# Retention layer and serf MLP on one core: two reorderings of the weight conversion and one of a scaling step

## The chip, the core and the metric

The kernel runs on one NeuronCore of a Trainium2 chip. Its time is the device time in microseconds; lower is better. The engines are named as the profile names them: PE (TensorE matmuls), PEld (TensorE weight loads), DVE (VectorE), ACT (ScalarE), POOL (GpSimd) and SP (SyncE, which issues nearly all of the DMAs here).

## The reference, cut to what matters

First a recurrent retention layer on q, k, v of shape (4, 8, 768, 64), then a two-layer MLP on its output seen as 3072 tokens by 512. Shortened:

```python
for t in range(S):                       # retention, per batch and head
    state = gamma * state + outer(k[t], v[t])
    y[t] = scale * q[t] @ state
x = y.transpose(0, 2, 1, 3).reshape(3072, 512)
h = x @ w_in                             # 512 x 2048, float64 in memory
g = h * erf(softplus(h))
out = g @ w_out                          # 2048 x 512, float64 in memory
```

The two weight matrices arrive as float64 and there is no float64 arithmetic in the kernel, so the kernel rebuilds a float32 from the two 32-bit words of every number.

## The kernel before

**Retention by chunks.** The sequence is cut into chunks of 128 positions, 24 in all (six for each batch). For chunk j the functions, with their short names, are: `ret_scale` (K_, one DVE multiplication of q and k by decay factors, L401), `ret_transpose` (T, PE transposes at L416 into two PSUM tiles, which ACT copies at L422 to qT and kT), `ret_scores` (S_, L429, two PSUM tiles), `ret_mask` (M, two DVE multiplications at L441 that read the two score tiles), `ret_out` (O_, matmuls at L464, L469 and L478 into two PSUM tiles, which ACT copies at L483), and `ret_add` (A, DVE adds to the running state from PSUM, L596). After the first four chunks all of these PSUM tiles come from one pool, `ps_r`, which has two buffers: each function that writes two tiles takes over the two that the function in front of it filled, so it has to wait until they have been read.

**Weights by pieces.** The weights come in 16 pieces of 1 MB, numbered 0 to 15, in the order in0, in1, in2, in3, out0, out1, in4, in5, out2, out3, in6, in7, out4, out5, out6, out7. `conversion(n)` is a Python generator that turns piece n to float32. From piece 2 on it has five steps, each with one DVE instruction on 128x1024 elements:

- step 1: L211 cuts out the exponent, and ACT scales it with a Relu (L212);
- step 2: L215 cuts out the upper mantissa (into a tile that all pieces share);
- step 3: L220 adds the lower word;
- step 4: L223 joins the sign to what ACT wrote at L212, and issues the DMA of the piece that takes the same raw buffer;
- step 5: L229 multiplies the two and writes the float32 weights.

The exponent tiles alternate between even and odd n, so step 1 of piece n+1 may run while piece n is unfinished.

**Order.** The program is written out by hand: each engine runs its instructions in the order in which Python records them. `weights()` lists the conversion steps of all pieces in one sequence. Every function of the retention and of the MLP calls `pace(n)`, which records the next n steps of that sequence at that place; `need(...)` records as many as are wanted for a certain weight. `pace_around(n)` records n/2 steps, then what stands in the list `waiting`, then n/2 steps. So `pace` decides where the conversion's DVE instructions stand among the others.

**MLP.** For the first 512 tokens there are four groups g of four hidden tiles. `hidden(g, u)` is the first layer for one tile (L649, ACT copy at L652); `gate(g)` runs softplus and erf on ACT (L609, L619, each with a table load); `gated(g)` multiplies on DVE (L638); `project(g, tt)` is the second layer (L663). In group g the order is hidden(g, 0 to 3), gate(g), project(g-1, 0 to 3), with the steps for chunks 4 and 5 put between by the table `after`. `project(0, 0)` needs pieces 4 and 5 (out0 and out1): its first two hidden tiles use piece 4, the other two use piece 5. The later 2560 tokens run from `hidden_part` (L720) and `project_part` (L792), with block products that need fewer multiplications.

Of the kernel before, what the change touches and what calls it, by code (L numbers as in the profile page):

```python
# [45 lines left out]
def kernel(  # L46
# [85 lines left out]
    def w_in_of(ft, kk):  # L132
        half, s, i = ft // (2 * FG), ft % (2 * FG) // FG, ft % FG
        return w_in_sb[:, s, 2 * half + kk // 2, kk % 2, i * P : (i + 1) * P]

    def w_out_of(ft):
        half, s, i = ft // (2 * FG), ft % (2 * FG) // FG, ft % FG
        return w_out_sb[:, s, 2 * half : 2 * half + 2, i, :]
# [11 lines left out]
    pieces = [("in", 0), ("in", 1)]  # L150
# [4 lines left out]
    n_p = len(pieces)  # L155
# [23 lines left out]
    def load_pieces_after(n):  # L179
        for later in range(n + 1, n_p):  # L180
            if place[later] == place[n]:
                load_piece(later)
                break

    def conversion(n):

        which, i = pieces[n]
        half, s, at = i // 4, i % 4 // 2, i % 2  # L190

        for part in range(2) if n < 2 else (None,):
            words = raws[place[n]].bitcast(U32)
            if which == "in":
                f = slice(at * 2 * P, (at + 1) * 2 * P)
                if part is not None:
                    f = slice((at * 2 + part) * P, (at * 2 + part + 1) * P)
                to = w_in_sb[:, s, 2 * half : 2 * half + 2, :, f].rearrange("p d k f -> p (d k) f")
            else:
                to = w_out_sb[:, s, 2 * half : 2 * half + 2, at * 2 : at * 2 + 2, :].rearrange(  # L200
                    "p d f c -> p d (f c)"
                )
            words = words.rearrange("p (a b w) -> p a b w", a=to.shape[1], w=2)
            number, power = (
                x.rearrange("p (a b) -> p a b", a=to.shape[1]) for x in (numbers, powers[n % 2])
            )
            if part is not None:
                f = slice(part * P, (part + 1) * P)
                words, number, power = words[:, :, f], number[:, :, f], power[:, :, f]
            lo, hi = words[:, :, :, 0], words[:, :, :, 1]  # L210
            nc.vector.tensor_scalar(power, hi, 0x7FF00000, None, op0=ALU.bitwise_and)  # L211
            nc.scalar.activation(power, power, AF.Relu, bias=below, scale=8.0)  # L212
            if part is None:
                yield
            nc.vector.tensor_scalar(  # L215
                number, hi, 0xFFFFF, 1 << 20, op0=ALU.bitwise_and, op1=ALU.bitwise_or
            )
            yield
            numberf = number.bitcast(F32)
            nc.vector.scalar_tensor_tensor(numberf, number, 2.0**32, lo, op0=ALU.mult, op1=ALU.add)  # L220
            if part is None:
                yield
            nc.vector.scalar_tensor_tensor(  # L223
                power, hi, 1 << 31, power, op0=ALU.bitwise_and, op1=ALU.bitwise_or
            )
            if part != 0:
                load_pieces_after(n)
            yield
            nc.vector.scalar_tensor_tensor(  # L229
                to, numberf, 2.0**-52, power.bitcast(F32), op0=ALU.mult, op1=ALU.mult,  # L230
            )
            done.update((which, 2 * i + u) for u in (range(2) if part is None else (part,)))
            yield

    def sums(which, s):

        if which == "in":
            assert all(("hidden", 2 * FG + s * FG + u) in done for u in range(FG))
            x = {name: w_in_sb[:, s, at] for name, at in IN.items()}
            of = (("S1", "21", "22", 1), ("S2", "S1", "11", 0), ("S3", "11", "21", 0), ("S4", "12", "S2", 0))  # L240
        else:
            assert ("project", s) in done
            x = {name: w_out_sb[:, s, at] for name, at in OUT.items()}
            of = (("T1", "12", "11", 0), ("T2", "22", "T1", 0), ("T3", "22", "12", 0), ("T4", "21", "T2", 0))
        for to, a, b, plus in of:
            nc.vector.tensor_tensor(x[to], x[a], x[b], op=ALU.add if plus else ALU.subtract)
            yield
        done.add(("sums " + which, s))
# [3 lines left out]
    def weights():  # L252


        before = iter(())
        for n in range(n_p):
            now = conversion(n)
            if n > 5:
                next(now)
                yield  # L260
            for _ in before:
                yield
            before = now
            if n and pieces[n - 1] == ("out", 5):
                yield from sums("in", 0)
        yield from before

    def later_sums():
        for which, n in (("in", 1), ("out", 0), ("out", 1)):
            yield from sums(which, n)  # L270

    weight_steps = weights()
    last_steps = later_sums()
    room = -1000.0

    def pace(n):

        nonlocal room
        room += n
        while room >= 1:  # L280
            next(weight_steps, None)
            room -= 1

    def need(*what):
        nonlocal room
        while what not in done:
            if next(weight_steps, done) is done:
                next(last_steps)
            room -= 1
# [13 lines left out]
    for n in range(1, 4):  # L303
# [6 lines left out]
        out=causal, in_=causal, compare_op=ALU.is_ge, fill=0.0,  # L310
# [293 lines left out]
    def gate(g):  # L604


        name = "r" if g < 4 and g % 2 else "e"
        E[g] = act.tile([P, N], F32, name=name, bufs=1)
        nc.scalar.activation(E[g], HS[g], AF.Softplus)  # L609

        if g:
            gate_erf(g)
# [8 lines left out]
    waiting = []  # L621

    def pace_around(n):


        pace(n / 2)
        run(waiting)
        waiting.clear()
        pace(n / 2)

    def run(steps):
        for f, *args in steps:
            f(*args)
# [8 lines left out]
    def hidden(g, u):  # L642
        ft = g * FG + u
        if u == 0:
            HS[g] = act.tile([P, N], F32, name="h")
        need("in", ft)
        p = ps_h.tile([P, TCH], F32, name="hp")
        for kk in range(n_k):
            nc.tensor.matmul(  # L649
                p, w_in_of(ft, kk), XC[0][:, kk, :], start=(kk == 0), stop=(kk == n_k - 1)  # L650
            )
        nc.scalar.copy(HS[g][:, u * TCH : (u + 1) * TCH], p)  # L652
        done.add(("hidden", ft))

        pace_around(3.4 if g > 1 else 2.5)

    def project(g, tt):
        if g == 0 and tt == 0:
            O[0] = [ps_o.tile([P, d_model], F32, name=f"o{i}") for i in range(TT)]
        need("out", g * FG + FG - 1)  # L660
        for u in range(FG):
            ft = g * FG + u
            nc.tensor.matmul(  # L663
                O[0][tt].rearrange("p (d c) -> p d c", d=2),
                E[g][:, u * TCH + tt * P : u * TCH + (tt + 1) * P],
                w_out_of(ft),
                start=(ft == 0),
                stop=(ft == n_ft - 1),
            )
        if tt == TT - 1:  # L670
            done.add(("project", g))
        pace_around(3.4)
# [16 lines left out]
    def chunk_of(g):  # L689
        return TCH // SCH + (g - G0) // 2  # L690
# [116 lines left out]
    def put_part(m, step):  # L807
# [27 lines left out]
    K_, T, S_, M, O_, A = (  # L835
        ret_scale, ret_transpose, ret_scores, ret_mask, ret_out, ret_add
    )
# [6 lines left out]
    for j in range(JPC):  # L844
# [8 lines left out]
        else:  # L853
# [19 lines left out]
            ([(S_, 4)], [(M, 4)]),  # L873
        ],
        [
            ([(O_, 4), (load, 6)], [(A, 4), (K_, 5)]),
            ([(T, 5), (load, 7)], []),
            ([(S_, 5)], [(M, 5)]),
            ([(O_, 5)], [(A, 5)]),
# [8 lines left out]
    for g in range(G0):  # L888
        for u in range(FG):

            if g and u == (2 if g == 1 else 0):
                waiting.append((gated, g - 1))
            hidden(g, u)
            run(after[g][u][0])
            waiting.extend(after[g][u][1])
        gate(g)
        if g:
            for tt in range(TT):
                project(g - 1, tt)

# [76 lines left out]
    g, m = NG - 1, chunk_of(NG - 1)  # L979
# [55 lines left out]
```

## Time and profile before

| | |
|---|---|
| median of 6 runs | 692.99 us (692.12 to 694.92) |
| the profiled execution | 692.96 us |
| its span, first to last instruction | 691.2 us |
| busy: PE, DVE, ACT, POOL | 678.8, 384.4, 257.3, 6.6 us |
| mean granted TensorE clock | 0.997 |
| mean DMA rate over the span | 68 GB/s |

The profile is of one execution. Its timeline gives, for each group of equal instructions, start, duration, engine, line, output and inputs, and in brackets the idle time of the engine before it with what ended that idle time. Times in the timeline count from the span's start. [...]

### The profile page before, as it was taken

Reading aid. Unit: us, or ns where it says so; the run is one execution under the profiler, and the core shown is the slowest. Engines: PE = TensorE matmul, PEld = TensorE weight load, DVE = VectorE, ACT = ScalarE, POOL = GpSimd, SP = SyncE. Lnnn points to the kernel's source line nnn. Section 1 sums busy time; section 2 is a strip of 40 time slices with the busy share of each in tenths; the row PEclk is TensorE's granted clock in tenths of the full one; section 3 lists DMA queues with packets and bytes.
Section 4 is the critical chain, followed back from the end, with each engine's and each line's share of the span. In section 5 each row is a group of like instructions: output and inputs, shape, how many; then the busy total and the mean of one; then the engine's idle time right before and its main releaser. Section 6 shows DMA issues by size and latency. Waiting matters only on the chain.

```text
span 691.2 us, 14344 instructions
## 1 busy us (share of the span) xinstructions
PE 678.8 (98%) x6214; PEld 578.7 (84%) x6214; DVE 384.4 (56%) x591; ACT 257.3 (37%) x293; POOL 6.6 (1%) x21
## 2 busy tenths in 40 slices
PE   8898999999999999999999999999999999999997
PEld 7644454486999999999999999999999999999996
DVE  4698999564863653563455455544544553343224
ACT  3267262425144144243342341441441432423430
POOL 2000000010000000000000000000000000000000
PEclk9999999999999999999999999999999999999999
DMA  9999963202321321222222222322221210000000
GB/s 193 216 233 241 195 202 84 39 1 38 105 44 35 75 48 31 63 46 43 67 43 45 69 39 46 72 36 44 50 58 34 49 43 1 2 32 1 1 31 32
DMA packets 147216, 47.12 MB, mean 68 GB/s; under 512 B 135760, under 2 KB 136016, under 8 KB 147152
## 3 DMA queue, kind: packets, MB, share of 16 engines
q1 hardware_dynamic: 144640, 45.66, 30.4%
q8 instruction: 49, 0.80, 0.5%
q10 hardware_dynamic: 2512, 0.53, 0.5%
q14 instruction: 15, 0.12, 0.1%
HBM read 39.86 MB, written 6.29 MB: 67 GB/s over the span
## 4 chain that ended last, share of the span: by engine, by line
PE 94%; DVE 2%; SPq 1%; DMA 1%; ACT 1%; issue 1%; DVEq 0%
PE hp L720 36%; PE o L792 35%; PE o L663 8%; PE hp L649 7%; PE r L528 1%; DMA e<-in_q_dram 1%; PE hp L493 1%; PE o L564 1%; SPq L119 1%; SPq L122 1%; PE r L416 1%; PE r L469 1%; PE hp L543 1%; PE r L543 1%; PE r L429 0%
## 5 line engine op out<-in xcount | busy, mean ns | idle before, releaser
L720 PE MATMUL hp<-xs,w_in_sb 128*128 128x128 f32 x1280 | 149.8, 275 | 0.0
L720 PEld LDWEIGHTS hp<-xs,w_in_sb 128*128 128x128 f32 x1280 | 147.8, 192 | 1.6 <-issue 0.5
L792 PE MATMUL o<-w_out_sb,h 128*128 128x256 f32 x640 | 141.7, 379 | 0.0
L792 PEld LDWEIGHTS o<-w_out_sb,h 128*128 128x128 f32 x640 | 121.6, 190 | 16.5
L720 PE MATMUL hp<-xT,w_in_sb 128*128 128x128 f32 x960 | 113.7, 275 | 0.0
L720 PEld LDWEIGHTS hp<-xT,w_in_sb 128*128 128x128 f32 x960 | 111.9, 192 | 1.9 <-issue 1.0
L792 PE MATMUL o<-w_out_sb,e 128*128 128x256 f32 x480 | 112.1, 383 | 0.0
L638 DVE TENSOR_TENSOR e<-h,e 128x1024 f32<-128x1024 f32 x42 | 49.6, 1222 | 102.7 <-ACT e L619 102.7
L792 PEld LDWEIGHTS o<-w_out_sb,e 128*128 128x128 f32 x480 | 88.2, 190 | 11.6
L649 PE MATMUL hp<-xT,w_in_sb 128*128 128x512 f32 x128 | 56.6, 595 | 0.8 <-DVE w_in_sb L229 0.7
L745 DVE TENSOR_TENSOR h<-h,hp 128x512 f32<-128x512 f32 x20 | 13.7, 687 | 75.3 <-PE hp L720 75.3
L609 ACT ACT_TABLE_LOAD x24 | 30.8, 1283 | 61.1 <-issue 45.4
L649 PEld LDWEIGHTS hp<-xT,w_in_sb 128*128 128x128 f32 x128 | 23.8, 190 | 29.8 <-issue 27.3
L619 ACT ACTIVATE e<-e 128x2048 f32<-128x2048 f32 (+1 forms) x23 | 42.1, 1836 | 0.2
L609 ACT ACTIVATE e<-h 128x2048 f32<-128x2048 f32 x22 | 42.0, 1911 | 0.2
L733 DVE TENSOR_TENSOR h<-h,hp 128x512 f32<-128x512 f32 x20 | 13.8, 688 | 46.5 <-PE hp L720 46.5
L743 ACT COPY h<-hp 128x512 f32<-128x512 f32 x20 | 11.7, 585 | 60.3 <-PE hp L720 60.3
L738 ACT COPY h<-hp 128x512 f32<-128x512 f32 x20 | 11.7, 586 | 57.9 <-PE hp L720 57.9
L736 ACT COPY h<-hp 128x512 f32<-128x512 f32 x20 | 11.7, 585 | 55.3 <-PE hp L720 55.3
L619 ACT ACT_TABLE_LOAD x24 | 30.8, 1283 | 0.4
L582 ACT COPY xT<-r 128x256 f32<-128x256 f32 x32 | 10.4, 375 | 54.8 <-PE r L528 54.8
L663 PE MATMUL o<-w_out_sb,e 128*128 128x512 f32 x64 | 28.2, 595 | 2.3 <-DVE w_out_sb L229 2.3
(134 smaller groups left out, 660.7 us busy)
## 6 DMA issues: line engine op xcount, KB each, us to landing
w_out_sb<-in_moe_w_out_dram SPq DMA_DIRECT2D x14, 512.0 KB, 5.7
w_in_sb<-in_moe_w_in_dram SPq DMA_DIRECT2D x12, 512.0 KB, 12.0
kq<-in_k_dram SPq DMA_DIRECT2D x23, 256.0 KB, 3.8
v<-in_v_dram SPq DMA_DIRECT2D x23, 256.0 KB, 3.1
out_dram<-r SPq DMA_DIRECT2D x23, 256.0 KB, 3.4
kq<-in_q_dram SPq DMA_DIRECT2D x256, 16.0 KB, 1.8
kb<-in_k_dram SPq DMA_DIRECT2D x256, 16.0 KB, 1.7
w_out_sb<-in_moe_w_in_dram SPq DMA_DIRECT2D x4, 512.0 KB, 10.7
```

The lines of the kernel that those rows point to most:

```text
L543: nc.tensor.matmul(other[a][own, u % 2, D:] if crossed else pp[a][own, u % 2, t], V[j][t, 2 * u + r, :], AM[j][t, r, u, :D], start=crossed ...
L609: nc.scalar.activation(E[g], HS[g], AF.Softplus)
L619: nc.scalar.activation(E[g][:, half], E[g][:, half], AF.Erf)
L638: nc.vector.tensor_tensor(E[g][:, half], HS[g][:, half], E[g][:, half], op=ALU.mult)
L649: nc.tensor.matmul(p, w_in_of(ft, kk), XC[0][:, kk, :], start=(kk == 0), stop=(kk == n_k - 1))
L663: nc.tensor.matmul(O[0][tt].rearrange("p (d c) -> p d c", d=2), E[g][:, u * TCH + tt * P : u * TCH + (tt + 1) * P], w_out_of(ft), start=(f ...
L720: nc.tensor.matmul(bank[:, u, :], w_in_sb[:, s, IN[a], kk, u * P : (u + 1) * P], XS[m][b][:, kk, :], start=(p in (1, 2, 5) and u == 0 and ...
L733: nc.vector.tensor_tensor(h["11"], h["11"], flat, op=ALU.add)
L736: nc.scalar.copy(h["12"], flat)
L738: nc.scalar.copy(h["22"], flat)
L745: nc.vector.tensor_tensor(h["12"], h["12"], flat, op=ALU.add)
L792: nc.tensor.matmul(O[m][i][:, half, :], G[g][a][:, u * P : (u + 1) * P], w_out_sb[:, s, OUT[b], u, :], start=i not in started, stop=(s == ...
```

## The change

There are three edits.

1. `weights()` places step 1 of piece n+1 differently. Before, from piece 6 on, step 1 of a piece stood in front of all remaining steps of the piece before it (for piece 6: in front of all five steps of piece 5). Now step 1 of piece n+1 stands between step 3 and step 4 of piece n, from piece 6 (the seventh) on.
2. `hidden(g, u)` calls `pace_around` with 3.4 steps from group 1 on, where group 1 had 2.5.
3. The scaling of chunk 5, the sixth (`K_` for 5), leaves the list that follows `hidden(2, 0)` and is put in the list that follows `project(0, 1)`, so that it is recorded in `project(0, 2)`.

```diff
@@ weights()
-        before = iter(())
-        for n in range(n_p):
-            now = conversion(n)
-            if n > 5:
-                next(now)
+        pending = [conversion(n) for n in range(n_p)]
+        begun = 0
+        for n, steps in enumerate(pending):
+            for k, _ in enumerate(steps, start=begun):
                 yield
-            for _ in before:
-                yield
-            before = now
-            if n and pieces[n - 1] == ("out", 5):
+                if n > 4 and n + 1 < n_p and k == 2:
+                    next(pending[n + 1])
+                    yield
+            begun = int(n > 4)
+            if pieces[n] == ("out", 5):
                 yield from sums("in", 0)
-        yield from before
@@ hidden(g, u)
-        pace_around(3.4 if g > 1 else 2.5)
+        pace_around(3.4 if g else 2.5)
@@ after
-            ([(O_, 4), (load, 6)], [(A, 4), (K_, 5)]),
+            ([(O_, 4), (load, 6)], [(A, 4)]),
@@ the loop over g
             for tt in range(TT):
                 project(g - 1, tt)
+                if g == 1 and tt == 1:
+                    waiting.append((K_, 5))
```

## The prediction

> **What bounds the kernel now.** I read the busy shares and the chain of waits on the page first, then the list of who waited for whom on PE after 60 us, then the chain and the timelines of the place that this list points to.
>
> ```profile
> PE 678.8 (98%) x6214; PEld 578.7 (84%) x6214; DVE 384.4 (56%) x591; ACT 257.3 (37%) x293; POOL 6.6 (1%) x21
> ...
> PE 94%; DVE 2%; SPq 1%; DMA 1%; ACT 1%; issue 1%; DVEq 0%
> ...
> PE o L663 <- DVE w_out_sb L229: 2.3, 1, 2.3
> PE r L416 <- issue: 0.6, 1, 0.6
> ```
>
> PE is full, so only a wait of PE can be won or added. After 60 us there are two in the whole run, and one is 2.3 us: `project(0, 0)` waits for the float32 weights of piece 5. How it comes about, from the chain, and below it the DVE timeline of the same place:
>
> ```profile
> 59.65 0.58 ACT h L652
> 60.23 1.05 ACT w_out_sb L212
> 61.28 1.04 ACT w_in_sb L212
> 62.33 0.02 issue
> 62.35 1.24 DVE w_in_sb L223
> 63.59 0.02 issue
> 63.61 1.24 DVE w_out_sb L229
> 64.84 0.04 issue
> 64.89 12.28 PE o L663 x28
> ```
>
> ```profile
> 56.89 0.69 DVE L211 TENSOR_SCALAR w_out_sb<-w_in_sb 128x1024 uint32<-128x1024 uint32 x1
> 57.49 0.69 DVE L211 TENSOR_SCALAR w_in_sb<-w_out_sb 128x1024 uint32<-128x1024 uint32 x1
> 58.09 0.69 DVE L215 TENSOR_SCALAR w_out_sb<-w_out_sb 128x1024 uint32<-128x1024 uint32 x1
> 58.81 1.23 DVE L220 SCALAR_TENSOR_TENSOR w_out_sb<-w_out_sb 128x1024 f32<-128x1024 uint32 x1
> 62.35 1.23 DVE L223 SCALAR_TENSOR_TENSOR w_in_sb<-w_out_sb,w_in_sb 128x1024 uint32<-128x1024 uint32 x1 [2.31 <-ACT w_in_sb L212]
> ```
>
> The first L211 is piece 6, the second piece 5. Both of their Relus stand on ACT behind the copy of `hidden(1, 3)`, which PE releases at 59.6, and piece 5's is second. So DVE stands still for 2.31 us and PE after it.
>
> **Part 1: the wait at 62 us.** In the changed program's order on each engine, DVE runs: L229 of piece 4, chunk 4's scaling, L211 and L215 of piece 5, the two gating multiplications, L220 of piece 5, L211 of piece 6, L223 and L229 of piece 5. ACT runs piece 5's Relu before the two copies of T(4), ahead of the copy of `hidden(1, 3)`. I replay DVE with the distances between starts in this trace: L211 to the next 0.60; L215 to L220 0.72; L220 to an independent one 1.15; L223 to L229 1.25; L229 to a dependent one 1.26, else 1.14; L401 1.13; the gating pair 2.27; the mask pair 1.20. From L220 of piece 4 at 49.94, which stays: L223 51.09, L229 52.34, L401 53.48, L211 54.61, L215 55.21, gating 55.81, L220 58.08, L211 of piece 6 59.23, L223 59.83, L229 61.08, its end (1.22 later) 62.30. PE waits in the trace until 0.06 after such an end: 62.36. PE itself, started at 60.63, needs four matmuls at 0.433 (28 of them take 64.89 to 77.01) and is ready at 62.36. The wait goes to nothing: PE gains 64.89 - 62.36 = 2.5 us.
>
> What moved later here is covered. Chunk 4's scaling ends at 54.7, and T(4) starts at 55.14. Gating ends at 58.2, wanted at 60.63. The T(4) copies come behind a Relu of 1.15 us, so they end at 58.0 instead of 56.9; S_(4) wants them at 59.54.
>
> **Part 2: what is late next.** Per piece the new order costs DVE the same: 0.72 + 1.15 + 0.60 + 1.25 + 1.26 = 4.98 against 5.00 (65.95 to 70.97, 70.97 to 75.95 in the trace). But 3.4 steps in group 1 and the earlier chunk 5 scaling put more DVE work in front of two instructions that PE waits for. Going on: mask of chunk 4 64.20, L223 of piece 6 66.00, piece 7 68.51, scaling of chunk 5 70.98 (its data landed at 62.4), piece 8 74.62, gating 78.22, piece 9 81.75, **A(4)** 83.61 to 84.03, L223 of piece 9 84.55, piece 10 87.06, L223 of piece 10 89.52, L215 of piece 11 92.03, **M(5)** 92.63 to 93.92.
>
> ```profile
> 83.14 0.42 DVE L596 TENSOR_TENSOR state<-state,r 128x256 f32<-128x256 f32 x1
> ...
> 86.16 1.04 PE L416 MATMUL r<-ident,kq 128*128 128x128 f32 x8
> ...
> 91.75 1.29 DVE L441 TENSOR_TENSOR am<-r,causal 128x512 f32<-128x512 f32 x2 [0.86 <-PE r L429]
> ...
> 95.28 0.67 PE L464 MATMUL r<-qT,state 64*64 64x128 f32 x16
> ```
>
> T(5) takes over the PSUM tile that A(4) reads. PE would be there at 86.16 - 2.53 = 83.63; A(4) is done at 84.1. A wait of 0.45. O_(5) writes both score tiles of chunk 5, so its second matmul waits for the second half of M(5): 93.92 + 0.06 = 93.98, where before it ran at 95.32. M(5) itself isn't held by PE (S_(5) ends by 89.6). The shift that is left is 95.32 - 93.98 = 1.34 us. The waits don't add up; M(5) is last and decides. In order of place: 2.5 won, 0.45 and 0.75 given back.
>
> **Part 3: behind M(5).** Here DVE and ACT run ahead. Weights of group 3 were ready at 101.6 and wanted at 110.74, and out5 at 112.5 against 124.48; both are now earlier on DVE. Piece 12's Relu now precedes `gate(2)`: its L211 ends near 95.8, so gate starts near 97.3, as before (97.47), and its product is wanted at 124.48.
>
> **The queues.** SP runs in order, and piece 12's two DMAs now stand before load(6), so that load waits for L223 of piece 8 (done 78.3 against an issue at 76.04 before). Chunk 6 is scaled at 125.55: nothing is lost. The other DMAs keep their order. Each raw piece lands before its L211: piece 8 at 66.8 against 70.38, piece 9 (issued up to 2 us earlier) before 70.6 against 76.48, pieces 10 and 11 are issued 1 to 2.5 us earlier than before, when they landed at 77.4 and 82.6, against 83.95 and 88.92. On ACT, piece 7's Relu comes after `gate(1)`, done near 68.7, wanted at 72.11; piece 10's precedes the T(5) copies, which end near 86.9, wanted near 88.5.
>
> Each L211 is now 4.2 us ahead of its L223 instead of 6.3, so the cover for ACT's work has shrunk, but by this count no Relu is late.
>
> **Sum.** 692.96 for the profiled execution less 1.3 is 691.7; the median shown, 692.99, gives the same.
>
> **A rule against it.** [...] Its columns are the stretch, its length, then busy time of PE, PEld, DVE, ACT, POOL, the granted clock and the DMA share:
>
> ```profile
> 18.64:22.05 3.41, 1.58 (x19) 1.23 (x15) 2.76 (x4) 0.45 (x1) 0.00 (x0) 1.00 1.17 204
> 22.05:25.46 3.41, 3.41 (x44) 3.08 (x45) 0.00 (x0) 0.62 (x2) 0.00 (x0) 0.50 1.06 215
> 61.50:65.00 3.50, 1.23 (x4) 0.30 (x3) 2.62 (x3) 3.47 (x3) 0.00 (x0) 1.00 0.99 295
> ```
>
> A stretch with PE 46% busy, with one wait of 1.83 us, was followed by 3.41 us at half clock, which is 1.7 us lost; the wait of 2.27 us at 62 us was not. So a wait near 1.8 us can cost 1.7 us on top, one of 0.75 leaves PE 78% busy. I count nothing, and keep the 1.7 for a rival.
>
> **Forecast, 0.60:** 691.7 us, own range 691.2 to 692.2 (the replay has about 30 distances, each good to 0.02 us, and the runs shown scatter by some tenths).
>
> **Rival 1, the whole gain, 0.17:** M(5) and A(4) are in time, and 2.5 us stay: 690.5. For it: DVE would need to be only 1.2 us faster than replayed. Against: the distances are regular, and the program has no other DVE gap before M(5) than the 2.31 and 0.86 us that the replay drops.
>
> **Rival 2, no effect, 0.17:** DVE is 0.6 to 2 us later than replayed (a Relu or a raw piece not in time), and O_(5) gives back nearly everything: 692.2 to 693.5, 693.0 in the middle. For it: DMAs are busy in nearly every slice up to 92 us, and piece 5 took 10.4 us to land where piece 8 took 5.8; with 10.4, piece 8 (issued at 61.0) would hold DVE at 71.4 instead of 70.38, which leaves 0.3 us of gain.
>
> **Rival 3, slower, 0.06:** the clock gate. If DVE comes to M(5) 1.05 us later than replayed, PE's wait before O_(5) grows to 1.8 us, as long as the one that halved the clock; 0.3 us of gain are left and 1.7 us are lost: 694.4. It decides from that point on. Against: it needs both the delay and the unlucky outcome of two seen.
>
> **How the numbers follow.** About 0.2% (1.39 us, so 691.6) is what a measurement of this kernel can tell from no change. The forecast lies just inside it; I put 0.45 of its chance below 691.6. Faster: 0.27 + 0.17 = 0.44. Same: 0.33 + 0.17 = 0.50. Slower: 0.06. The range 690.4 to 692.9 holds the forecast, rival 1 and the nearer half of rival 2.
>
> **What would show it.** Right: no wait of PE on L229 near 62 us; `project(0, 0)` in one run of 32 matmuls; DVE without a gap from 50 to 94 us; a PE wait of about 0.45 us before T(5), put to L596, and about 0.75 us before O_(5), put to L441; L464 there starting near 93.3. Wrong: a DVE gap before an L211 or L223 between 65 and 92 us, M(5) before 91.5 or after 94, a half clock after 93 us, or a new PE wait behind 97 us, which the replay only covers by slack.

## The result, and the profile after

| | before | changed |
|---|---|---|
| median | 692.46 us (690.38 to 694.92, 70 runs) | 689.87 us (688.92 to 692.03, 33 runs) |
| profiled execution: time, span | 692.96, 691.2 us | 690.46, 688.7 us |
| mean granted clock in it | 0.997 | 1.000 |

The ratio is 0.9967 (95% interval 0.9960 to 0.9974), so 2.3 us or 0.33% faster, clear of no change; the two medians differ by 2.6. The forecast was 691.7 with a range of 690.4 to 692.9. The measured time lies half a microsecond below that range: the direction was right, the size was half of what came.

First the waits of PE after 50 us in the changed kernel (total, number, longest, in us), then its PE timeline at the same places. In what is shown here, its line numbers above 265 are one less than those of the kernel before: L662 is the old L663.

```profile
PE r L463 <- DVE am L440: 0.7, 2, 0.5
PE r L415 <- issue: 0.6, 1, 0.6
```

```profile
57.90 1.16 PE L428 MATMUL r<-qT,kT 64*128 64x128 f32 x16
58.99 14.35 PE L662 MATMUL o<-w_out_sb,e 128*128 128x512 f32 x32
73.17 3.60 PE L648 MATMUL hp<-xT,w_in_sb 128*128 128x512 f32 x8
...
82.32 1.14 PE L415 MATMUL r<-ident,kq 128*128 128x128 f32 x8
...
86.83 1.16 PE L428 MATMUL r<-qT,kT 64*128 64x128 f32 x16
...
92.12 0.43 PE L463 MATMUL r<-qT,state 64*64 64x128 f32 x2 [0.50 <-DVE am L440]
92.71 0.66 PE L463 MATMUL r<-qT,state 64*64 64x128 f32 x14 [0.17 <-DVE am L440]
...
94.33 14.00 PE L662 MATMUL o<-w_out_sb,r 128*128 128x512 f32 x32
108.17 13.90 PE L648 MATMUL hp<-xT,w_in_sb 128*128 128x512 f32 x32
```

The same stretch in the kernel before, from S_(5) to `project(1, 0)`:

```profile
90.56 1.16 PE L429 MATMUL r<-qT,kT 64*128 64x128 f32 x16
...
96.91 14.00 PE L663 MATMUL o<-w_out_sb,r 128*128 128x512 f32 x32
```

`project(0, 0)` now runs through as 32 passes, and the wait on piece 5 is gone from the list of waits. From start to start these passes still take 14.18 us (58.99 to 73.17), where the 32 of `project(1, 0)` take 13.84: 0.34 us of the wait are left in this profile. The list of waits doesn't show them, only the listed durations do, 14.35 us against 14.00. A pass of `project(1, 0)` is listed with 0.595 us on average, but the next starts after 0.43 (13.84 / 32), so I go by the starts. A new wait stands before O_(5), put to the mask of chunk 5, as the forecast said. The list gives it 0.50 + 0.17 us. Here too the starts say more: from S_(5) to `project(1, 0)` pass 7.50 us, in the kernel before 6.35, so the wait costs 1.15 us. The DVE timeline:

```profile
48.63 1.23 DVE L220 SCALAR_TENSOR_TENSOR w_out_sb<-w_out_sb 128x1024 f32<-128x1024 uint32 x1
...
57.93 0.68 DVE L211 TENSOR_SCALAR w_out_sb<-w_in_sb 128x1024 uint32<-128x1024 uint32 x1
58.53 1.21 DVE L223 SCALAR_TENSOR_TENSOR w_in_sb<-w_out_sb,w_in_sb 128x1024 uint32<-128x1024 uint32 x1
59.77 1.23 DVE L229 SCALAR_TENSOR_TENSOR w_out_sb<-w_out_sb,w_in_sb 128x1024 f32<-128x1024 f32 x1
...
82.33 0.41 DVE L595 TENSOR_TENSOR state<-state,r 128x256 f32<-128x256 f32 x1
...
91.38 1.28 DVE L440 TENSOR_TENSOR am<-r,causal 128x512 f32<-128x512 f32 x2
```

From L220 of piece 4 to M(5) are 42.75 us; the replay had 49.94 to 92.63, 42.69. So the order of work did what it was counted to do. What does not fit is the start of the stretch: the changed kernel's S_(4) is on PE at 57.90, the old one's was at 59.54, and nothing of the change lies ahead of that point but a few DVE and ACT steps with slack. At `project(1, 0)` the two stand at 94.33 and 96.91. Of 2.58 us, then, 1.64 were there before the edited stretch began, and 0.94 came inside it. The 1.64 fit the half-clock stretch at 22 us, which the profiled run of before had and that of after did not (22.05 to 25.46: granted clock 0.50 and 1.00). One pair of profiles thus shows less than the forecast inside the edited stretch, while the medians show more. The experiments had to explain both.

### The profile page after: what moved, and what is told of

Read it like the earlier page. It is cut to its first block, busy times and chain, and to the rows that moved or that the text cites. A ratio compares the mean times of both kernels' runs of the same rounds, so it can differ in the third digit from the quotient of the medians.

```text
span 688.7 us, 14344 instructions
## 1 busy us (share of the span) xinstructions
PE 679.0 (99%) x6214; PEld 578.3 (84%) x6214; DVE 384.3 (56%) x591; ACT 257.7 (37%) x293; POOL 6.6 (1%) x21
## 4 chain that ended last, share of the span: by engine, by line
PE 86%; DVE 7%; DMA 2%; issue 2%; SPq 2%; ACT 0%; DVEq 0%
PE hp L719 36%; PE o L791 36%; PE o L662 6%; PE hp L648 2%; PE r L527 1%; PE hp L492 1%; DMA e<-in_q_dram 1%; DVE w_out_sb L215 1%; PE o L563 1%; DMA w_out_sb<-in_moe_w_out_dram 1%; DVE w_out_sb L223 1%; SPq L119 1%; DVE w_out_sb L220 1%; DVE w_in_sb L229 1%; DVE w_in_sb L223 1%
## 5 line engine op out<-in xcount | busy, mean ns | idle before, releaser
L742 ACT COPY h<-hp 128x512 f32<-128x512 f32 x20 | 11.7, 585 | 60.3 <-PE hp L719 60.3
L737 ACT COPY h<-hp 128x512 f32<-128x512 f32 x20 | 11.7, 585 | 57.9 <-PE hp L719 57.9
L735 ACT COPY h<-hp 128x512 f32<-128x512 f32 x20 | 11.7, 585 | 55.3 <-PE hp L719 55.3
L730 ACT COPY h<-hp 128x512 f32<-128x512 f32 x20 | 11.7, 587 | 48.3 <-PE hp L719 48.3
```

Source lines behind the costliest of these rows:

```text
L730: nc.scalar.copy(h["11"], flat)
L735: nc.scalar.copy(h["12"], flat)
```

## The experiments

Theory A: the granted clock takes part. Theory B: all 2.3 us are the reordering itself. Each run comes with its mean granted clock, so runs can be sorted. A stretch like the one in the profile of before, 3.41 us at 0.50, takes 1.7 of some 690 us, or 0.0025, from the mean. By this estimate a run of 0.999 or 1.000 has no such stretch (it is called full clock below), and one of 0.998 or less is taken to have at least one. One exception is met below.

**The changed kernel again**, beside the kernel before.

> The changed kernel itself, once more, beside the kernel before on one chip, with the granted clock of every run. Theory A (clock): a half-clock stretch of 3.4 us near 22 us of the span hits some runs of either kernel and costs those about 1.3 to 1.7 us; between runs with the same mean clock (1.00 or 0.997) the change is worth 1.0 to 1.5 us. Theory B (all of it is the reordering): runs with equal clock differ by 2.3 to 2.6 us.

Measured: 690.05 against 691.81 us, ratio 0.9973 (0.9961 to 0.9984). Over all the sets with the kernel before beside them (this one and those below), with the runs of the changed kernel from three sets (34 of the result that have a clock on record, 12 here and 10 below):

| mean clock of the run | kernel before | changed kernel |
|---|---|---|
| 0.999 or 1.000 | 26 runs, median 690.76 us | 55 runs, median 689.96 us |
| 0.998 or less | 53 runs, median 692.63 us | 1 run, 692.03 us |

At full clock the change is worth 0.8 us, below theory A's 1.0 to 1.5 and far below theory B's 2.3. The other part is the number of runs that lose clock: 53 of 79 before, 1 of 56 after, at 1.9 us each. Theory A as written took the half clock for chance, alike for both kernels. That was wrong: with the change it is all but gone.

**More matmuls in the gap at 19 us, before and after.** The edit in both kernels:

```diff
+        if j == 2:
+            keep_warm(6)
         if j + 1 < JPC:
             T(j + 1)
```

> The kernel before with six more unused 128x128 matmuls before T(3), in the PE gap of 1.6 to 1.8 us near 19 us, so that PE is busy about 80% of that window instead of 46%. Theory A: no half clock near 22 us, and the median falls by about 1.5 us to 690.7 to 691.2, with the wait of 2.3 us on piece 5's weights still there. Theory B: no change beyond 0.3 us, 692.3 to 692.9.

> The changed kernel with the same six matmuls before T(3). Theory A: the changed kernel as measured (689.9) had the full clock in most runs, so it stays within 0.3 us of it; against the kernel before with the same matmuls it is 1.0 to 1.5 us faster. Theory B: it is 2.3 to 2.6 us faster than that kernel.

Measured: 692.66 us for the kernel before with them, ratio 1.0007 (0.9991 to 1.0022), where theory A expected 690.7 to 691.2. Seven of its 12 runs still lost clock. The changed kernel with them: 690.26 us, all 11 runs at full clock. The two differ by 2.4 us, which by the medians alone is what theory B expected; at full clock they differ by 0.7. The gap was filled (PE is busy all of 18.6 to 22.0 us in that profile), so it isn't where the loss comes from in most runs. The profile of the first shows a place where it does. Columns of this view: stretch, length, busy PE, PEld, DVE, ACT, POOL, granted clock, DMA share, GB/s.

```profile
59.50:62.90 3.40, 1.16 (x3) 0.19 (x1) 2.65 (x4) 3.37 (x3) 0.00 (x0) 1.00 1.13 174
62.90:66.40 3.50, 3.47 (x4) 1.47 (x5) 3.46 (x5) 3.47 (x3) 0.00 (x0) 0.52 0.90 327
66.40:69.80 3.40, 3.40 (x9) 1.52 (x8) 3.33 (x5) 1.52 (x3) 0.00 (x0) 1.00 0.90 288
```

```profile
58.67 1.98 PE L663 MATMUL o<-w_out_sb,e 128*128 128x512 f32 x4
62.93 13.98 PE L663 MATMUL o<-w_out_sb,e 128*128 128x512 f32 x28 [2.27 <-DVE w_out_sb L229]
76.75 3.60 PE L649 MATMUL hp<-xT,w_in_sb 128*128 128x512 f32 x8
```

The wait that the change removes, 2.27 us, left PE a third busy in a stretch of 3.4 us (1.16 of 3.40), and the next 3.5 us ran at a granted clock of 0.52. The 28 passes took 62.93 to 76.75, 13.82 us, against 12.12 in the profile of before: beyond the wait itself, 1.70 us were lost. In the forecast's profile the same wait was not followed by a half clock (1.00 from 64.89 to 68.30).

**The wait kept, but PE busy in it.** Theory A2: this wait is what halves the clock. The edit to the kernel before, in `project(0, 0)` ahead of the third hidden tile:

```diff
+            if ft == 2 and tt == 0:
+                for _ in range(10):
+                    nc.tensor.matmul(O[0][3][:, :P], ident, ident, start=True, stop=True)
```

> The kernel before with twenty unused 128x128 matmul passes (about 2.2 us) inside the wait of project(0,0) for piece 5, so that the wait keeps its length but PE is busy in it. Theory A2 (the removed wait was paid twice, once as 2.3 us of standing still and in about 6 of 10 runs again as 3.4 us at half clock): clock 1.00 or 0.999 in nearly all runs and a median of 690.8 (span 689.0), 1.0 to 1.7 us under the kernel before. Rival: the low clock comes from elsewhere (the prologue near 22 us, or chance): the share of low-clock runs stays and the median stays within 0.4 us of the kernel before.

Measured: 691.35 us against 692.30; 10 of 12 runs at full clock (0.999 or 1.000), where the kernel before beside it had 12 of 35. The ratio is 0.9991 (0.9978 to 1.0004), so by itself not a clear gain, and the median is 0.5 us above the 690.8 that was expected: its runs at full clock have a median of 691.1, those of the kernel before 690.8, and where these 0.3 us go isn't settled. What decides is the count of runs. The PE timeline shows that the wait was only filled:

```profile
60.53 1.98 PE L666 MATMUL o<-w_out_sb,e 128*128 128x512 f32 x4
62.35 2.39 PE L665 MATMUL o<-ident 128*128 128x128 f32 x20
64.78 12.28 PE L666 MATMUL o<-w_out_sb,e 128*128 128x512 f32 x28
```

The 28 passes start at 64.78, within 0.11 us of the kernel before (64.89), whose profiled run lost clock in the same place: this run too is one of the two with lost clock (0.998), and the half clock lies in the prologue, from about 22.3 us on: its S_(4) starts at 59.44, that of the changed kernel at 57.90. That is the second place.

**The new place of step 1 alone** (edit 1 of the three).

> The new place of step 1 alone, with 2.5 steps in group 1 and the scaling of chunk 5 where it was. Replay: piece 5's Relu is first behind the copy of hidden(1,3), done at 61.3; L229 of piece 5 ends at 63.8; PE waits 1.2 us instead of 2.3. M(5) stands two steps earlier than in the changed kernel and holds nothing. At full clock 1.0 to 1.1 us under the kernel before: 689.7. If a wait of 1.2 us is too short to halve the clock, the median is 689.7 to 690.0, as fast as the whole change; if it does, 690.5 to 691.2.

Measured: 689.93 us, ratio 0.9970 (0.9956 to 0.9985): as fast as the whole change. Its chain has piece 5's Relu first behind the copy of `hidden(1, 3)`, and the wait is halved, as replayed:

```profile
56.94 0.59 ACT h L651
57.52 1.06 ACT w_in_sb L212
58.58 0.02 issue
58.60 1.24 DVE w_in_sb L223
59.84 0.02 issue
59.86 1.24 DVE w_out_sb L229
61.10 0.04 issue
```

PE waits 1.24 us, M(5) holds nothing, and 10 of 12 runs kept the full clock. So with a wait of 1.24 us at this place 2 of 12 runs lost clock, with one of 2.27 us 53 of 79. Whether the two runs that lost it did so here or in the prologue isn't known; the profiled run is not one of them.

**Edits 1 and 2, with chunk 5's scaling where it was.**

> Edits 1 and 2 without moving the scaling of chunk 5. Replay: the wait at 62 us goes (2.5 us won), but the scaling of chunk 5 now stands behind A(4) and ends about 86.7 (in the count of the kernel before), so T(5) waits about 3 us. At full clock about 0.5 us slower than the kernel before, 691.3; and with a wait long enough to halve the clock 692 to 693. Rival: the scaling isn't wanted so early and its place does nothing: as the changed kernel, 689.9.

Measured: 692.18 us, ratio 1.0000 (0.9986 to 1.0015). The wait at 62 us is gone from the list, and the next one is as long:

```profile
PE r L415 <- DVE kq L400: 2.3, 1, 2.3
```

```profile
82.45 1.22 DVE L400 TENSOR_TENSOR kq<-kq,kq_s 128x1024 f32<-128x1024 f32 x1
```

```profile
83.92 1.06 PE L415 MATMUL r<-ident,kq 128*128 128x128 f32 x8 [2.27 <-DVE kq L400]
```

With 3.4 steps in group 1 the scaling of chunk 5 comes so late that T(5) stands still for it. The six runs at full clock have a median of 691.3 us (690.6 to 692.1), which the replay had. So edit 3 exists to pay for edit 2. The other six have 0.998 or less, and here is the exception: the profiled one has 0.998, but before the end its clock is full, and the half clock lies in the last 2.6 us (687.9 to 690.5, clock 0.50), when the last matmul is done (at 685.3) and only the last stores are under way. It cost PE nothing; this run is long because 4.7 us passed from its last DVE instruction to the end, where the changed kernel's profile has 3.3. In the changed kernel, which ends in the same way, one of 56 runs reads so low, so few of the 53 runs counted above can be of this kind.

**Edits 2 and 3, without the new place of step 1.**

> Edits 2 and 3 without the new place of step 1. Replay: with more steps in group 1 both Relus of pieces 6 and 5 come before the T(4) copies on ACT, piece 5's weights are done at 62.4 and the wait of PE at 62 us is under 0.2 us all the same; M(5) holds PE before O_(5) as in the changed kernel. So within 0.3 us of the changed kernel, 689.6 to 690.2: the new place of step 1 alone isn't what removes the wait. Rival: step 1's place is needed, and 1 us or more of the wait stays: 691 or more.

Measured: 693.86 us, ratio 1.0021 (1.0007 to 1.0036), slower than before, and 4 us above what I expected; 8 of 12 runs lost clock. DVE, ACT and PE of that kernel:

```profile
56.34 0.69 DVE L211 TENSOR_SCALAR w_out_sb<-w_in_sb 128x1024 uint32<-128x1024 uint32 x1 [3.00 <-DMA w_in_sb<-in_moe_w_in_dram]
```

```profile
57.07 1.15 ACT L212 ACTIVATE w_out_sb<-w_out_sb,below 128x1024 uint32<-128x1024 uint32 x1 [3.03 <-DVE w_out_sb L211]
...
59.63 0.58 ACT L422 COPY qT<-r 128x512 f32<-128x512 f32 x1
```

```profile
60.26 2.08 PE L429 MATMUL r<-qT,kT 64*128 64x128 f32 x16 [2.35 <-ACT qT L422]
62.27 14.60 PE L663 MATMUL o<-w_out_sb,e 128*128 128x512 f32 x32
```

The part that I expected came: `project(0, 0)` is one run of 32, so the wait on piece 5 goes without edit 1 too. But a new one of the same length stands in front of S_(4), and a half clock followed it here (0.52 over 60 to 63 us): S_(4) took 2.01 us from start to start instead of 1.09. Step 1 of piece 6 stands in front of all of piece 5, and with the faster pace DVE reaches it at 53.3, 3.0 us before the raw data of piece 6 have landed. DVE waits, ACT's Relu waits, and behind it in ACT's queue the copies of T(4), for which PE waits 2.35 us. The new place of step 1 puts piece 6's first step behind L211, L215, the gating and L220 of piece 5, at 57.93 in the changed kernel, after the landing. That cover I had checked for the changed kernel and forgotten for this one.

**The mask of chunk 5 directly behind its scores**, in the changed kernel:

```diff
-            ([(S_, 5)], [(M, 5)]),
+            ([(S_, 5), (M, 5)], []),
```

> The changed kernel with the mask of chunk 5 recorded directly behind the scores, in front of the conversion steps that follow hidden(2,3), so some 2 to 3 us earlier on DVE. If M(5) holds PE before O_(5) as its trace says (0.50 + 0.17 us), that wait goes and 0.6 to 0.8 us are won: 689.1 to 689.3. If the wait is not on the path that sets the end, the time stays at 689.9.

> The changed kernel with the mask of chunk 5 directly behind its scores, once more, with more runs. Its trace has no PE wait on that mask any more. If that wait (0.67 us) is all that went, 0.6 to 1.1 us under the changed kernel of the same chip, full clock in nearly all runs: 688.9 to 689.4. Rival: the 688.97 seen before was chance, and it is within 0.3 us of the changed kernel.

> The changed kernel beside it, for comparison on the same chip: 689.7 to 690.2, with full clock (0.999 or 1.0) in nearly all runs, where the kernel before has it in about 4 of 10.

Measured: 688.97 and 688.72 us on two chips, with the changed kernel beside them at 690.05 and 690.11. The second has a ratio of 0.9942 (0.9924 to 0.9961) to the kernel before. DVE and PE of the first:

```profile
88.55 1.28 DVE L440 TENSOR_TENSOR am<-r,causal 128x512 f32<-128x512 f32 x2
```

```profile
85.98 1.16 PE L428 MATMUL r<-qT,kT 64*128 64x128 f32 x16
...
90.70 0.67 PE L463 MATMUL r<-qT,state 64*64 64x128 f32 x16
...
92.32 14.00 PE L662 MATMUL o<-w_out_sb,r 128*128 128x512 f32 x32
```

M(5) is done at 89.8, O_(5) comes at 90.70 and runs without a wait. So the wait was on the path, and this version beats both kernels. The medians differ by 1.1 and 1.4 us, more than the 0.67 us that the list of waits gave and that I had expected to win. The starts account for most of it: from S_(5) to `project(1, 0)` pass 6.34 us here, practically as in the kernel before, and 7.50 in the changed kernel. Three of its 13 runs lost clock; the one of them that was profiled did so in the prologue (clock 0.51 from 22.10 to 25.50).

## Why the prediction was wrong, step by step

**Part 1, the wait at 62 us: right.** By starts, `project(0, 0)` lost 2.54 us in the kernel before (60.63 to 77.01 is 16.38, against 13.84), as forecast. In the changed kernel 0.34 us of it stay in the profile of the result and in the one taken beside the mask-first version, nothing in that of the changed kernel again. Edit 1 alone halves the wait; edits 2 and 3 alone remove it and put another in its place.

**Part 2, what is late next: right as a sum, not in its terms.** T(5) was to cost 0.45 us and M(5) 0.75. T(5) started at 82.32, while A(4) ran from 82.33 to 82.74: its first half doesn't wait for A(4). From T(5) to the next group passed 0.98 us instead of 0.87, so 0.11 us. M(5) took 1.15 and covered the difference: 1.26 against 1.20. M(5) decides what is left, for removing its wait won time.

**The sum at equal clock: right in two profiles of four.** From S_(4) to `project(1, 0)` the profile of before has 37.37 us, and the one with matmuls in the gap 39.06 - 1.70 = 37.36. The changed kernel has 36.10 when run again and 36.12 with matmuls in the gap: a gain of 1.26, where 1.3 was forecast. It has 36.43 in the profile of the result and 36.44 in the one beside the mask-first version, a gain of 0.94. In these two DVE waited 0.31 and 0.57 us at 47 us for the raw data of piece 4, and the whole chain up to M(5) came later against PE. The medians at full clock differ by 0.8; the rest isn't explained.

**The failed step is "A rule against it".** I had the half clock in hand, with its price of 1.7 us, and laid it only against the new waits. That these would cost no clock was my estimate, from the 78% of PE that a wait of 0.75 us leaves busy; in the profile after, PE is 80% busy around the wait before O_(5) (2.73 of 3.40 us, 91.40 to 94.80), and the clock is 1.00 there and in the 3.4 us behind it. Of the wait that the change removes I wrote that it "was not" followed by a half clock, and counted nothing: one execution, taken for the rule. The clock of 53 of 79 runs of the kernel before says that a half-clock stretch lies somewhere, and filling the wait at 62 us brought that to 2 of 12. The missing term is about 1.87 us (692.63 less 690.76) in 0.67 of the runs before against 1 run in 56 after, 1.2 us on average. With 0.8 that makes 2.0 us in the mean; the medians of those same runs, 692.39 and 689.97, differ by 2.4, because the median before lies among the runs with lost clock. What stays open is the prologue: its program is the same in all kernels but the two with matmuls in the gap, three of the twelve profiles show a half clock there, and yet the changed kernel lost clock in only 1 of 56 runs.

**Rival 1** came nearest to the measured number (690.5) by luck: its reason is refuted, for M(5) was not in time. **Rival 3** had the right mechanism, on the wrong side. **Rival 2**, a late raw piece, happened in the changed kernel only with the 0.31 and 0.57 us of piece 4, but with 3.0 us in edits 2 and 3 alone.

**The base of the sum.** The profiled run of before had its half clock at 22 us and none at 62 us. Subtracting from its 692.96 took a run that lost clock as the base and left that loss in the result. The kernel before at full clock has 690.76; less 1.3 that is 689.5, and 689.96 was measured at full clock.

## What to carry to other kernels

The wait of PE at 62 us had two prices: its length, 2.54 us from start to start, and in some runs the clock behind it, 1.70 us in the profile that shows it. When a change removes or shortens a wait, sort the runs by granted clock and count both, since a single profile shows only one outcome. And when a pace is raised, look for the next instruction that is pushed back: here two of the three edits are only worth having together with the others, and the first alone gives the same time.

## What the runs showed of the hardware

In three profiles the stretch ahead of a half clock has PE partly busy: 34% (1.16 of 3.40 us) in the kernel before with matmuls in the gap, then 3.5 us at 0.52; 46% (1.58 of 3.41 us) in the prologue of the kernel before, then 3.41 us at 0.50; 50% (1.69 of 3.40 us) in the prologue of the second profile of the version with the mask first, then 3.40 us at 0.51. As little doesn't always bring it: 35% (1.23 of 3.50 us, 61.50 to 65.00) in the profile of before and 54% (1.85 of 3.41 us, 18.64 to 22.05) in that of after were both followed by 3.4 us at 1.00. The same wait differs from run to run: with 2.3 us at 62 us 53 of 79 runs lost clock, with the same wait filled by unused matmuls 2 of 12, with 1.2 us there 2 of 12, in the changed kernel 1 of 56. The small counts can't be put to the shorter waits: the version with the mask first has neither wait and lost clock in 3 of 13. What decides between the two outcomes of the same wait no run here shows.
